# Tiny softmax instructions moved to ScalarE, and the first pairs' sums made by TensorE products

## The chip, the cores and the metric

The kernel runs on one core of a Trainium2 chip. The metric is the device time of one execution in microseconds; before the change the median of three runs is 959.35 us (959.06 to 961.71). Engines are named by their usual names: TensorE (PE in the profile; PEld is its weight load), VectorE (DVE), ScalarE (ACT), GpSimd (POOL) and the queue of SyncE (SP), which issues the DMAs.

## The reference

Three stages over 2304 tokens (4 batches of 576, 8 heads of 64 channels). The attention adds a coarse and a local part; then come two feed-forward layers.

```
q_d, k_d, v_d = means of q, k, v over groups of 4 tokens        # 144 of 576
out_d   = softmax(scale * q_d k_d^T) v_d ;  out_up = repeat(out_d, 4)
out_loc = softmax(scale * q k^T where |i - j| < 4, else -1e9) v
attn    = out_up + out_loc              # each softmax divides by (sum + 1e-9)
x = (h - tanh(h)) @ w_out,   h = attn @ w_in                      # 512 -> 2048 -> 512
y = (sigmoid(x @ w_gate) * (x @ w_val)) @ w_out2                  # 512 -> 1536 -> 512
```

All of it is fp32 in and out.

## The kernel before, in words

**Tiles and order.** Two heads make a pair (128 partitions); a pair is called (batch, number), and there are 16 of them. The tokens are also cut in six chunks of 384 for the first feed-forward layer, where for each chunk 16 blocks `f` of `h` (`do_h`, lines 650 to 658) and of `y` (`do_y`, 660 to 672) follow each other, `y` two blocks behind. Each block is 4 by 3 wide products (128x384), since weights and activations are split in a high and a low part (`mm3`, 283). The weights `w1` come in as 64-bit words, and ScalarE and VectorE make the two parts from them (`w_begin` 224, `w_bits` 236, `w_high` 244, `w_low` 254).

**Attention items.** The attention is a list of items (560 to 571): `("d", pair)` is the coarse part of a pair (`down`, 353), `("l", pairs, block)` the local part of six blocks of 64 tokens (`local`, 431). An item issues its first products at once and puts the rest on later steps: `down` the maximum 2 steps later (`top`), the exponentials 3 (`exps`), the division 5 (`normalise`, 340), the transposes 7 and 8 (`turn`), the products with v 10 (`values`).

**Steps.** `tick` (140) counts steps; `defer`, `chain` and `later` file work under a step. An h or y block is two steps. In the first chunk (`dense[0]`) `work` (763) starts item i when step `begin + 60 * (i - first) / (goal - first)` has come and the item before has had its 4 ("d") or 6 ("l") steps (`item`, 594). `fetch` (582) loads the next pair when the sums of the last have been taken up (`means`), and files their sums four steps later (`load_pair`, 318). Before the dense part of chunk 1 the loop at 938 steps on until all attention output of that chunk is stored.

**Sums of four tokens.** For a pair, `mean_qk` (324) makes the sums of q and k in one tile `m`: batch 0 by one VectorE reduction (328), the others by three GpSimd additions (330 to 332). `mean_v` (334) makes the sums of v with three GpSimd additions from the buffer `vr` (one for all pairs) into `vd`. `down` multiplies the summed q by the summed k (364) and the exponentials by the summed v (415). An fp32 product is two instructions in the profile.

**Tiny instructions.** In `down`, `top` ends with a VectorE product that scales the negated maxima, `nb` (383, 128x3). `normalise` begins with a VectorE instruction that adds 1e-9 to the sums and multiplies them (342, 128x3 or 128x6), then the reciprocal (346) and the product (348).

**The start.** Until the four x tiles of chunk 0 exist (742 to 757) each round issues unused products with the identity (`keep_warm`, 735; line 738): two at its head and, while fewer than eight items have been started, two more. The rest of each round is one item, some early h products and two steps. The place `spot` (697) holds q and k of pair (0,3) in its first 1152 of 4096 columns.

**Who keeps what order.** GpSimd keeps the program's order at the start (692), SP in chunk 0 (927), SP, ScalarE, VectorE and GpSimd in chunks 1 to 5 (929). TensorE is ordered by the compiler's scheduler up to the end of the first layer, ScalarE and VectorE up to the end of chunk 0. The kernel runs what is in each queue in its order.

Of the kernel before, what the change touches and what calls it, by code (L numbers as in the profile page):

```python
# [7 lines left out]
F32 = mybir.dt.float32  # L8
# [4 lines left out]
ACTF = mybir.ActivationFunctionType  # L13
ALU = mybir.AluOpType
AX = mybir.AxisListType
# [3 lines left out]
B, H, S, D = 4, 8, 576, 64  # L19
NP = H // 2  # L20
FAC = 4
SD = S // FAC
# [7 lines left out]
WIN = QB + 2 * (FAC - 1)  # L30
LB = 6
# [27 lines left out]
def tile_kernel(ctx: ExitStack, tc: tile.TileContext, qk, vp, v, w1, w2, mask, ident, out):  # L59
    nc = tc.nc  # L60
    scale = 1.0 / float(D) ** 0.5
# [11 lines left out]
    ap = pool("ap", 1, p1)  # L73
# [15 lines left out]
    startup, dense, spare = [True], [True], [0]  # L89
# [4 lines left out]
    def a_bank():  # L94

        spare[0] += 1
        if startup[0] and spare[0] % 5 == 2:
            return acc_bank(1)
        return ps.tile([128, 512], F32, tag="ab", bufs=4, name="ab")
# [6 lines left out]
    now = [0]  # L106
# [23 lines left out]
    def chain(n, fn, *args):  # L130

        chains.setdefault(now[0] + n, []).append(fn(*args))
# [156 lines left out]
    qks, means, vds, outd = {}, {}, {}, {}  # L289
# [20 lines left out]
        nc.sync.dma_start(out=qks[u], in_=qk[u[0], u[1]])  # L310

    def load_v(u):
        vds[u] = ap.tile([72, 2, 128], F32, tag="vd", bufs=2, name="vd")
        vr = ap.tile([72, 2, FAC, 128], F32, tag="vr", name="vr")
        nc.sync.dma_start(out=vr, in_=vp[u[0], u[1]])
        return vr

    def load_pair(u, d):
# [2 lines left out]
        defer(d, mean_qk, u)  # L321
        defer(d, mean_v, u, vr)

    def mean_qk(u):
        m = means[u] = ap.tile([128, 2, SD], F32, tag="m", bufs=1, name="m")
        t = qks[u].rearrange("p i (j r) -> p i j r", r=FAC)
        if u[0] == 0:
            nc.vector.tensor_reduce(out=m, in_=t, op=ALU.add, axis=AX.X)
        else:
            nc.gpsimd.tensor_tensor(out=m, in0=t[:, :, :, 0], in1=t[:, :, :, 1], op=ALU.add)  # L330
            nc.gpsimd.tensor_tensor(out=m, in0=m, in1=t[:, :, :, 2], op=ALU.add)
            nc.gpsimd.tensor_tensor(out=m, in0=m, in1=t[:, :, :, 3], op=ALU.add)

    def mean_v(u, vr):
        vd = vds[u]
        nc.gpsimd.tensor_tensor(out=vd, in0=vr[:, :, 0, :], in1=vr[:, :, 1, :], op=ALU.add)
        nc.gpsimd.tensor_tensor(out=vd, in0=vd, in1=vr[:, :, 2, :], op=ALU.add)
        nc.gpsimd.tensor_tensor(out=vd, in0=vd, in1=vr[:, :, 3, :], op=ALU.add)

    def normalise(pt, ssum, n, w, mul):  # L340
        r = ssum
        nc.vector.tensor_scalar(
            out=r, in0=ssum, scalar1=1e-9, scalar2=mul, op0=ALU.add, op1=ALU.mult
        )
        yield
        nc.vector.reciprocal(out=r, in_=r)
        yield
        nc.vector.tensor_tensor(
            out=pt, in0=pt, in1=r.unsqueeze(2).to_broadcast([128, n, w]), op=ALU.mult
        )  # L350


    def down(u):
        m = means.pop(u)
        qd, kd = m[:, 0, :], m[:, 1, :]
        four = not startup[0]
        sd = score_banks(3 * SD, 2 * SD, SD)
        place = [(j % 2, j // 2) if four else (0, j) for j in range(3)]
        for j in range(3):
            for h in range(2):  # L360
                r0 = 64 * h
                t, at = place[j]
                o0 = 64 - r0 if t else r0
                nc.tensor.matmul(  # L364
                    out=sd[t][o0:o0 + 64, at, :], lhsT=qd[r0:r0 + 64, 40 * j:40 * j + 64],
                    rhs=kd[r0:r0 + 64, :], start=True, stop=True,
                )
        sc = scale / (FAC * FAC)
        nb = ap.tile([128, 3], F32, tag="nb", bufs=2, name="nb")
        pd = ap.tile([128, 3, SD], F32, tag="pd", bufs=1, name="pd")  # L370
        ssum = ap.tile([128, 3], F32, tag="ss", bufs=2, name="ss")
        pdt = ap.tile([72, 2, 2, 3, 48], F32, tag="pdt", name="pdt")
        b, p = u
        if p % 2 == 0:
            outd[b, p // 2] = ap.tile([128, 2, SD], F32, tag="od", bufs=2, name="od")
        od = outd[b, p // 2]

        def top():
            for t in range(len(sd)):
                at = nb[:, t::2] if four else nb  # L380
                nc.vector.tensor_reduce(out=at, in_=sd[t], op=ALU.max, axis=AX.X, negate=True)
                yield
            nc.vector.tensor_scalar_mul(nb, nb, sc)

        def exps():
            for j in range(3):
                nc.scalar.activation(
                    out=pd[:, j, :], in_=sd[place[j][0]][:, place[j][1], :], func=ACTF.Exp, bias=nb[:, j:j + 1], scale=sc,
                    accum_out=ssum[:, j:j + 1],
                )  # L390

        def turn(f):
            if f == 0:
                defer(1, run_later, "d")
            tb = a_bank()[:72, :384]
            for j in range(3):
                nc.tensor.transpose(  # L397
                    out=tb[:, 128 * j:128 * j + 128], in_=pd[:, j, 72 * f:72 * f + 72], identity=id_sb
                )

            if not four:
                kept = bass.AP(tensor=tb.tensor, offset=tb.offset, ap=[list(tb.ap[0]), [64, 2], [136, 3], [1, 48]])
                defer(1, copy, pdt[:, f], kept)
                return
            outer = bass.AP(tensor=tb.tensor, offset=tb.offset, ap=[list(tb.ap[0]), [64, 2], [272, 2], [1, 48]])
            defer(1, copy, pdt[:, f, :, ::2, :], outer)
            for h in range(2):
                defer(1, copy, pdt[:, f, h, 1, :], tb[:, 200 - 64 * h:248 - 64 * h])

        def values():  # L410
            vd = vds.pop(u)
            ob = a_bank()[:, :SD]
            for h in range(2):
                for f in range(2):
                    nc.tensor.matmul(  # L415
                        out=ob[64 * h:64 * h + 64, :], lhsT=vd[:, f, 64 * h:64 * h + 64],
                        rhs=pdt[:, f, h].rearrange("p j k -> p (j k)"), start=(f == 0), stop=(f == 1),
                    )
            defer(1, copy, od[:, p % 2, :], ob)

        chain(2, top)
        defer(3, exps)
        chain(5, normalise, pd, ssum, 3, SD, float(FAC))
        wait = 0 if dense[0] else 2
        defer(7, turn, 0)
        defer(8, turn, 1)
        later("d", 10 + wait, values)

    def local(us, n):
        b, p = us[0]
# [5 lines left out]
        for x in (0, 3, 1, 4, 2, 5):  # L438
            i, j = blocks[x]
            t = qks[us[i]]  # L440
            w0 = win_start(j)
            for h in range(2):
                r0 = 64 * h
# [3 lines left out]
                    out=bank[o0:o0 + 64, at, :], lhsT=t[r0:r0 + 64, 0, QB * j:QB * j + QB],  # L447
                    rhs=t[r0:r0 + 64, 1, w0:w0 + WIN], start=True, stop=True,
# [6 lines left out]
        pl = ap.tile([128, LB, WIN], F32, tag="pl", bufs=2, name="pl")  # L455
        nb = ap.tile([128, LB], F32, tag="nl", bufs=2, name="nb")
        ssum = ap.tile([128, LB], F32, tag="sl", bufs=2, name="ss")
# [46 lines left out]
        def exps():  # L504
            for j in range(LB):
                nc.scalar.activation(  # L506
                    out=pl[:, j, :], in_=pl[:, j, :], func=ACTF.Exp, bias=nb[:, j:j + 1],
                    accum_out=ssum[:, j:j + 1],
                )

        def turn(f):
            if f == 0:
# [39 lines left out]
        defer(1, load_window)  # L552
        chain(2, top)
        defer(3, exps)
        chain(7, normalise, pl, ssum, LB, WIN, 1.0)
        defer(9, turn, 0)
        defer(10, turn, 1)
        later("l", 12, values)
# [35 lines left out]
    def item():  # L594

        fetch()
        x = items[started[0]]
        if x[0] == "d" and x[1] not in means:
            return 0
        started[0] += 1  # L600
        run_later()
        if x[0] == "d":
            down(x[1])
            return 4 if dense[0] else 7
        local(*x[1:])
        return 6 if dense[0] else 7
# [94 lines left out]
    vr = load_v((0, 0))  # L701
# [33 lines left out]
    def keep_warm(n):  # L735

        for _ in range(n):
            nc.tensor.matmul(out=idle[:, :128], lhsT=id_sb, rhs=id_sb, start=True, stop=True)  # L738
# [1 line left out]
    idle = acc_bank(0)  # L740
    free, rounds = [0], 0
    while any(((1, 0), k) not in xt for k in range(KD)):
        keep_warm(2)
        if started[0] < n_first:
            x = items[started[0]]
            item()
            if x[0] == "d":
                next_pair(x[1][1])
        early_h(2)
        tick()  # L750
        if started[0] < n_first:
            keep_warm(2)
        w_load(min(loaded[0] + 1, 3))
        rounds += 1
        if rounds % 3 == 0:
            w_begin(U1)
        tick()
# [388 lines left out]
```

## Time and profile before

| | us |
|---|---|
| median of three runs | 959.35 (959.06 to 961.71) |
| the profiled execution | 960.45 |
| its span, first to last instruction | 958.6 |
| TensorE busy | 934.3 (97%) |
| VectorE busy | 548.4 (57%) |
| ScalarE busy | 433.2 (45%) |
| GpSimd busy | 104.1 (11%) |

The profile is of one execution. A row of the time-line gives the start in us, the length in us, the engine, the line and the operation, the tile written and the tiles read, and in brackets the time that the engine had stood idle and what ended it. TensorE's instructions overlap: each lasts longer than the distance to the next one's start. The granted clock of TensorE is given as a share of 2.4 GHz, 0.5 being the lower of its two levels.

### The profile page before, as it was taken

The numbers are of one execution on the slowest core, as the hardware profiler recorded it, in microseconds if no ns is written. First come the engines' busy times: TensorE is split into PE (matmuls) and PEld (weight loads), VectorE is DVE, ScalarE is ACT, GpSimd is POOL, SyncE is SP. The second block draws the span as 40 slices with busy tenths as digits, with TensorE's granted clock in tenths as the row PEclk, the third lists the DMA queues.
The fourth block names the chain that finished last, engine by engine and source line by source line (L and its number), as shares of the span: only waits on it lengthen the run. The fifth ranks groups of instructions, "written<-read, shape, count | busy, mean of one in ns | idle before, by whom it ended". The sixth has DMA issues, their size and how long they took to land.

```text
span 958.6 us, 16060 instructions
## 1 busy us (share of the span) xinstructions
PE 934.3 (97%) x6260; PEld 867.8 (91%) x6260; DVE 548.4 (57%) x992; ACT 433.2 (45%) x1104; POOL 104.1 (11%) x113
## 2 busy tenths in 40 slices
PE   7888999999999999999999999999999998999998
PEld 6677989999999989999999999999999997888886
DVE  6897966344443534474346578585777676532231
ACT  4875755444543444452344545344443544422131
POOL 2243130302212020000033210000000000000000
PEclk9898999999999999999999999999999999999999
DMA  8475643212323120430121223142231445444341
GB/s 281 143 243 174 238 118 114 71 33 73 89 64 88 54 76 12 147 122 25 48 68 59 67 99 136 52 154 88 100 118 73 150 179 188 122 139 125 115 132 66
DMA packets 49963, 106.53 MB, mean 111 GB/s; under 512 B 5136, under 2 KB 35552, under 8 KB 45536
## 3 DMA queue, kind: packets, MB, share of 16 engines
q1 hardware_dynamic: 49888, 105.51, 33.3%
q8 instruction: 49, 0.80, 0.4%
q14 instruction: 26, 0.21, 0.1%
HBM read 77.97 MB, written 27.53 MB: 110 GB/s over the span
## 4 chain that ended last, share of the span: by engine, by line
PE 88%; DVE 3%; ACT 3%; DMA 2%; POOL 2%; issue 1%; SPq 0%; ACTq 0%; POOLq 0%; DVEq 0%
PE ab L284 14%; PE ab L286 14%; PE ab L285 14%; PE acc L284 13%; PE acc L285 12%; PE acc L286 12%; PE ab L525 2%; PE ab L446 1%; PE ab L516 1%; PE ab L397 1%; PE acc L738 1%; DMA qk<-in_qk 1%; PE ab L415 1%; PE ab L364 1%; ACT pl L506 1%
## 5 line engine op out<-in xcount | busy, mean ns | idle before, releaser
L297 DVE TENSOR_TENSOR t<-ab,t 128x384 f32<-128x384 f32 x94 | 52.2, 556 | 150.6 <-ACT t L640 150.4
L284 PE MATMUL acc<-g,w 128*128 128x384 f32 x384 | 133.2, 348 | 0.0
L284 PE MATMUL ab<-x,w 128*128 128x384 f32 x376 | 131.5, 350 | 1.2 <-DVE t L297 0.7
L285 PE MATMUL acc<-g,w 128*128 128x384 f32 x384 | 129.6, 337 | 0.0
L286 PE MATMUL acc<-g,w 128*128 128x384 f32 x384 | 129.5, 337 | 0.0
L285 PE MATMUL ab<-x,w 128*128 128x384 f32 x376 | 127.2, 338 | 0.0
L286 PE MATMUL ab<-x,w 128*128 128x384 f32 x376 | 127.2, 338 | 0.0
L640 ACT ACTIVATE t<-ab 128x384 f32<-128x384 f32 x94 | 45.8, 487 | 156.4 <-PE ab L286 155.3
L284 PE MATMUL acc<-x,f 128*128 128x384 f32 x252 | 84.8, 336 | 0.0
L286 PE MATMUL acc<-x,f 128*128 128x384 f32 x252 | 84.6, 336 | 0.0
L286 PE MATMUL ab<-x,f 128*128 128x384 f32 x252 | 84.6, 336 | 0.0
L285 PE MATMUL acc<-x,f 128*128 128x384 f32 x252 | 84.6, 336 | 0.0
L284 PE MATMUL ab<-x,f 128*128 128x384 f32 x252 | 84.6, 336 | 0.0
L285 PE MATMUL ab<-x,f 128*128 128x384 f32 x252 | 84.6, 336 | 0.0
L297 DVE TENSOR_TENSOR g<-t,g 128x384 fp32r<-128x384 f32 x96 | 59.8, 624 | 42.4 <-ACT g L294 40.1
L279 DVE TENSOR_TENSOR g<-u,g 128x384 fp32r<-128x384 f32 x72 | 38.6, 556 | 66.0 <-ACT g L294 65.9
L284 PEld LDWEIGHTS ab<-x,w 128*128 128x128 f32 x376 | 71.2, 189 | 4.5 <-issue 1.6
L284 PEld LDWEIGHTS acc<-g,w 128*128 128x128 f32 x384 | 72.2, 188 | 2.7 <-issue 1.8
L285 PEld LDWEIGHTS acc<-g,w 128*128 128x128 f32 x384 | 72.5, 189 | 0.3 <-issue 0.2
L286 PEld LDWEIGHTS acc<-g,w 128*128 128x128 f32 x384 | 72.3, 188 | 0.3 <-issue 0.2
L285 PEld LDWEIGHTS ab<-x,w 128*128 128x128 f32 x376 | 71.4, 190 | 0.0
L286 PEld LDWEIGHTS ab<-x,w 128*128 128x128 f32 x376 | 71.3, 189 | 0.1
(137 smaller groups left out, 1878.7 us busy)
## 6 DMA issues: line engine op xcount, KB each, us to landing
raw<-in_w SPq DMA_DIRECT2D x34, 1024.0 KB
u<-c SPq DMA_DIRECT2D x36, 384.0 KB
u<-u SPq DMA_DIRECT2D x72, 192.0 KB
qk<-in_qk SPq DMA_DIRECT2D x16, 576.0 KB
vr<-in_vp SPq DMA_DIRECT2D x16, 288.0 KB
y<-y SPq DMA_DIRECT2D x24, 192.0 KB
xs<-y SPq DMA_DIRECT2D x24, 192.0 KB
out<-o SPq DMA_DIRECT2D x17, 256.0 KB
```

The source lines that it names most:

```text
L279: nc.vector.tensor_tensor(out=dst[:, 1, :], in0=src, in1=dst[:, 0, :].bitcast(F32), op=ALU.subtract)
L284: nc.tensor.matmul(out=o, lhsT=wh, rhs=xh, start=first, stop=False, **kw)
L285: nc.tensor.matmul(out=o, lhsT=wh, rhs=xl, start=False, stop=False, **kw)
L286: nc.tensor.matmul(out=o, lhsT=wl, rhs=xh, start=False, stop=last, **kw)
L297: nc.vector.tensor_tensor(out=dst, in0=a, in1=b, op=ALU.subtract)
L364: nc.tensor.matmul(out=sd[t][o0:o0 + 64, at, :], lhsT=qd[r0:r0 + 64, 40 * j:40 * j + 64], rhs=kd[r0:r0 + 64, :], start=True, stop=True,)
L397: nc.tensor.transpose(out=tb[:, 128 * j:128 * j + 128], in_=pd[:, j, 72 * f:72 * f + 72], identity=id_sb)
L415: nc.tensor.matmul(out=ob[64 * h:64 * h + 64, :], lhsT=vd[:, f, 64 * h:64 * h + 64], rhs=pdt[:, f, h].rearrange("p j k -> p (j k)"), start ...
L446: nc.tensor.matmul(out=bank[o0:o0 + 64, at, :], lhsT=t[r0:r0 + 64, 0, QB * j:QB * j + QB], rhs=t[r0:r0 + 64, 1, w0:w0 + WIN], start=True, ...
L506: nc.scalar.activation(out=pl[:, j, :], in_=pl[:, j, :], func=ACTF.Exp, bias=nb[:, j:j + 1], accum_out=ssum[:, j:j + 1],)
L525: nc.tensor.matmul(out=ob[r0:r0 + 64, QB * x:QB * x + QB], lhsT=vw[0][:, j - n, i, r0:r0 + 64], rhs=pt[:, x, o0:o0 + 64], start=True, stop ...
L640: nc.scalar.activation(out=t, in_=hb[:, :N], func=ACTF.Tanh)
```

## The change

- The scale of `nb` and the guard of the sums become ScalarE activations (`Copy` with a scale and a bias), issued with the exponentials.
- For batch 0 `mean_v` does nothing, and `values` multiplies by the four unsummed v of each group and accumulates: 8 products per head where there were 2. The v of pairs (0,1) and (0,2) get a place of their own in `spot`.
- For pairs (0,1) to (0,3) `mean_qk` sums k only, and `down` multiplies the four unsummed q of each group by the summed k and accumulates: 24 products where there were 6.
- In the first chunk a "d" item is not started until five steps after its sums were issued.
- `keep_warm` issues two products at a round's head until three items have been started and one from then on, and two more in a round only until then.

```diff
     def load_v(u):
-        vds[u] = ap.tile([72, 2, 128], F32, tag="vd", bufs=2, name="vd")
-        vr = ap.tile([72, 2, FAC, 128], F32, tag="vr", name="vr")
+        if u[0] == 0 and u[1] in (1, 2):
+            vr = vds[u] = spot[:72, 2 * S + 1024 * (u[1] - 1):2 * S + 1024 * u[1]].rearrange(
+                "k (f r c) -> k f r c", f=2, r=FAC
+            )
+        else:
+            vr = ap.tile([72, 2, FAC, 128], F32, tag="vr", name="vr")
+            vds[u] = vr if u[0] == 0 else ap.tile([72, 2, 128], F32, tag="vd", bufs=2, name="vd")
...
     def mean_qk(u):
+        summed[u] = now[0]
...
         if u[0] == 0:
-            nc.vector.tensor_reduce(out=m, in_=t, op=ALU.add, axis=AX.X)
+            first = 1 if u[1] else 0
+            nc.vector.tensor_reduce(out=m[:, first:], in_=t[:, first:], op=ALU.add, axis=AX.X)
...
     def mean_v(u, vr):
+        if u[0] == 0:
+            return
...
-    def normalise(pt, ssum, n, w, mul):
+    def guard(ssum, mul):
+        nc.scalar.activation(out=ssum, in_=ssum, func=ACTF.Copy, scale=mul, bias=1e-9 * mul)
+
+    def normalise(pt, ssum, n, w):
         r = ssum
-        nc.vector.tensor_scalar(
-            out=r, in0=ssum, scalar1=1e-9, scalar2=mul, op0=ALU.add, op1=ALU.mult
-        )
-        yield
...
-        for j in range(3):
+        whole = qks[u][:, 0, :].rearrange("p (j r) -> p r j", r=FAC)
+        spread = u[0] == 0 and u[1] > 0
+        for j in range(3) if spread else ():
+            for r in range(FAC):
+                for h in range(2):
+                    r0 = 64 * h
+                    nc.tensor.matmul(
+                        out=sd[0][r0:r0 + 64, j, :], lhsT=whole[r0:r0 + 64, r, 40 * j:40 * j + 64],
+                        rhs=kd[r0:r0 + 64, :], start=(r == 0), stop=(r == FAC - 1),
+                    )
+        for j in range(3) if not spread else ():
...
-            nc.vector.tensor_scalar_mul(nb, nb, sc)
 
         def exps():
+            nc.scalar.activation(out=nb, in_=nb, func=ACTF.Copy, scale=sc)
             for j in range(3):
...
+            guard(ssum, float(FAC))
...
+            parts = [(f, r) for f in range(2) for r in range(FAC)] if u[0] == 0 else [(0, None), (1, None)]
             for h in range(2):
-                for f in range(2):
+                for x, (f, r) in enumerate(parts):
+                    vt = vd[:, f, :] if r is None else vd[:, f, r, :]
                     nc.tensor.matmul(
-                        out=ob[64 * h:64 * h + 64, :], lhsT=vd[:, f, 64 * h:64 * h + 64],
-                        rhs=pdt[:, f, h].rearrange("p j k -> p (j k)"), start=(f == 0), stop=(f == 1),
+                        out=ob[64 * h:64 * h + 64, :], lhsT=vt[:, 64 * h:64 * h + 64],
+                        rhs=pdt[:, f, h].rearrange("p j k -> p (j k)"), start=(x == 0), stop=(x == len(parts) - 1),
                     )
...
-        if x[0] == "d" and x[1] not in means:
+        if x[0] == "d" and (x[1] not in means or now[0] < summed[x[1]] + (5 if dense[0] and not startup[0] else 0)):
             return 0
...
-        keep_warm(2)
+        keep_warm(2 if started[0] < 3 else 1)
...
         if started[0] < n_first:
-            keep_warm(2)
+            keep_warm(2 if started[0] < 3 else 0)
```

In `local`, `exps` likewise ends with `guard(ssum, 1.0)`.

## Rows read from the trace of the kernel before

**Rows 1.** The page, part 1: busy time, share of the span, instructions.

```profile
PE 934.3 (97%) x6260; PEld 867.8 (91%) x6260; DVE 548.4 (57%) x992; ACT 433.2 (45%) x1104; POOL 104.1 (11%) x113
```

**Rows 2.** Busy by stretch: from:to, length, PE, PEld, DVE, ACT, POOL, granted clock, DMA.

```profile
50.00:126.00 76.00, 67.55 (x599) 59.48 (x599) 68.57 (x110) 52.06 (x147) 27.50 (x24) 0.96 0.59 199
22.00:29.30 7.30, 7.30 (x104) 5.58 (x104) 7.12 (x14) 5.53 (x18) 3.35 (x3) 1.00 0.55 168
29.30:37.00 7.70, 4.73 (x61) 3.54 (x61) 6.35 (x15) 7.70 (x36) 3.06 (x3) 0.86 0.70 235
37.00:50.00 13.00, 13.00 (x121) 10.00 (x121) 10.15 (x15) 10.77 (x18) 0.00 (x0) 0.82 0.38 123
...
70.40:82.60 12.20, 7.97 (x56) 7.12 (x56) 7.81 (x13) 4.51 (x11) 4.15 (x4) 0.72 0.50 172
82.60:126.00 43.40, 41.85 (x380) 36.94 (x380) 41.30 (x66) 33.51 (x96) 13.43 (x12) 1.00 0.56 190
...
146.50:700.00 553.50, 552.53 (x3849) 535.13 (x3848) 305.12 (x590) 244.49 (x652) 60.46 (x66) 1.00 0.24 79
```

**Rows 3.** Waits of TensorE: who waited for whom, us in total, times, longest.

```profile
PE ab L364 <- POOL m L332: 4.2, 1, 4.2
PE ab L525 <- ACT pt L294: 3.0, 2, 2.6
PE ab L516 <- DVE pl L348: 1.9, 1, 1.9
```

**Rows 4.** Time-line of TensorE and GpSimd, 69 to 75.8 us.

```profile
69.97 0.49 PE L516 MATMUL ab<-id_sb,pl 128*70 128x128 f32 x3
74.69 0.71 PE L364 MATMUL ab<-m 64*64 64x144 f32 x12 [4.23 <-POOL m L332]
...
73.69 0.94 POOL L332 TENSOR_TENSOR m<-m,qk 128x288 f32<-128x288 f32 x1
```

**Rows 5.** Time-line of TensorE: two wide products that follow each other.

```profile
144.47 0.34 PE L284 MATMUL ab<-x,w 128*128 128x384 f32 x1
144.65 0.34 PE L285 MATMUL ab<-x,w 128*128 128x384 f32 x1
```

**Rows 6.** Lines 342, 383: ns min/median/max; busy 50:126 (342, then 383); neighbours.

```profile
L342 DVE TENSOR_SCALAR ss<-ss x40: 155/164/1584, 10.4 to 389.8; 128x6 f32<-128x6 f32 x24, 128x3 f32<-128x3 f32 x16
...
L383 DVE TENSOR_SCALAR nb<-nb x16: 158/273/735, 8.7 to 356.8; 128x3 f32<-128x3 f32 x16
...
50.00:126.00 76.00, 4.34 (x8) 0.96 0.59 199
...
50.00:126.00 76.00, 1.55 (x3) 0.96 0.59 199
...
58.11 0.93 DVE L342 TENSOR_SCALAR ss<-ss 128x6 f32<-128x6 f32 x1
...
L695 ACT ACTIVATE z<-z 128x1 f32<-128x1 f32 x1 | 0.2, 203 | 0.0
```

**Rows 7.** The start: VectorE's sums by line, then time-line and chain.

```profile
L328 DVE TENSOR_REDUCE m<-qk 128x288 f32<-128x1152 f32 x4 | 5.4, 1349 | 6.6 <-DMA qk<-in_qk 4.9 <-PE acc L364 1.5
...
18.12 0.95 PE L364 MATMUL acc<-m 64*64 64x144 f32 x12
...
22.43 0.74 PE L415 MATMUL ab<-pdt,vd 72*64 72x144 f32 x8
...
29.29 0.41 ACT L294 ACTIVATE pdt<-ab 72x288 f32<-72x288 f32 x1 [1.40 <-PE ab L397]
...
39.02 0.99 PE L284 MATMUL acc<-x,w 128*128 128x384 f32 x2
...
19.07 3.10 PE acc L738 x26
```

**Rows 8.** Weight loads by line and shape: busy us, mean ns; 64 and 128 columns.

```profile
L364 PEld LDWEIGHTS acc<-m 64*64 64x64 f32 x24 | 1.4, 132 | 0.3 <-ACT pd L387 0.3
...
L285 PEld LDWEIGHTS acc<-g,w 128*128 128x128 f32 x384 | 72.5, 189 | 0.3 <-issue 0.2
```

More of the change, by code (lines that the diff above doesn't have):

```diff
@@ L322, in load_pair @@
         defer(d, mean_v, u, vr)
+    summed = {}
     def mean_qk(u):
+        summed[u] = now[0]
         m = means[u] = ap.tile([128, 2, SD], F32, tag="m", bufs=1, name="m")
@@ L422, in down @@
         defer(3, exps)
-        chain(5, normalise, pd, ssum, 3, SD, float(FAC))
+        chain(5, normalise, pd, ssum, 3, SD)
         wait = 0 if dense[0] else 2
@@ L509, in exps @@
                 )
+            guard(ssum, 1.0)
         def turn(f):
@@ L554, in local @@
         defer(3, exps)
-        chain(7, normalise, pl, ssum, LB, WIN, 1.0)
+        chain(7, normalise, pl, ssum, LB, WIN)
         defer(9, turn, 0)
```

## The prediction

> **What bounds the kernel now.** I read the page's head first, then busy time by stretch, then TensorE's list of waits, then the time-line around the longest of them. The head: TensorE is busy 934.3 of 958.6 us [rows 1], so almost every microsecond is TensorE work, and a change can win only where TensorE idles, runs at the lower clock, or multiplies something nobody uses. The stretches show where that is. From 146.5 to 700 us TensorE is busy 552.53 of 553.50 us at full clock [rows 2]: nothing that only touches VectorE or ScalarE there can move the end. All the room lies in the first 126 us. Two stretches there have a granted clock below 1, and since the clock has two levels (1.2 and 2.4 GHz) the time at the lower one can be worked out: (1 - 0.72) x 12.20 / 0.5 = 6.8 us in 70.4 to 82.6, and (1 - 0.86) x 7.70 / 0.5 + (1 - 0.82) x 13.00 / 0.5 = 6.8 us between 29.3 and 50.
>
> Three waits stand out [rows 3]: 4.2 us for GpSimd's `m` (the summed q and k of a pair), 2.6 us for a ScalarE copy, 1.9 us for a VectorE normalisation. The first two precede the two falls of the clock. The time-line of the first shows the mechanism [rows 4]: TensorE has issued its last transposes at 69.97, next in its queue are the products of pair (1,1), and they wait until GpSimd's last addition (73.69, 0.94 long) ends. TensorE takes its queue in order, so the wide products behind stood still too. In 82.6 to 126 VectorE is busy 41.30 of 43.40 us beside TensorE's 41.85 [rows 2]: that stretch has two bounds close together, and what TensorE wins earlier can be taken back there.
>
> **Part 1: five steps from sums to products.** Counting steps through the planner's code: in the first chunk ten items are spread over 60 steps, six apart. Pair (1,0) has its sum in step 53 and its products in 60: untouched. Pair (1,1) has both in step 65; now its products wait for step 70. The items behind it move by three (74, 80, 86; (1,2) in 92, already 15 steps behind its sum, now 17). (1,3) is summed in 97 and multiplied in 102 (before: 94 and 95), and the last item of the chunk moves from 101 to 106, the loads of chunk 1 from step 116 to 121. A step is half an h or y block, six wide products; they start 0.18 apart [rows 5], so 1.1 us. Five steps put 5.4 us of products into a hole of 4.2 us: the wait goes (-4.2), and with it the fall of the clock, 6.8 us in which TensorE did half of what it could (-3.4). The steps added at the end of the chunk hold no dense work of their own; blocks 14 and 15 and the last y blocks can be drawn ahead, since TensorE is not kept to program order here. SP is kept to it: the load of chunk 1 stays behind the last item's store and the weight loads stay behind that load, so if the cover is too thin the start of chunk 1 is late. I take 0 and keep +3 for the range.
>
> **Part 2: tiny instructions to ScalarE.** L342 (40 of them) and L383 (16) leave VectorE. Their median is 164 and 273 ns, but the longest took 1584 and 735 [rows 6]: in 50 to 126 eight and three of them took 4.34 + 1.55 = 5.9 us, 0.54 each. On ScalarE the nearest row is the 128x1 activation, 0.20 us; with both the guard and the scale waiting for the value just before them I take 0.2 to 0.4 each. After 126 us this is all hidden by TensorE. In 50 to 126 VectorE loses 5.9 us and ScalarE gains 11 x 0.2 to 0.4 = 2 to 4 us, and ScalarE has the room (33.51 of 43.40 us busy [rows 2]). The wait of 1.9 us for the normalisation [rows 3] had an L342 of 0.93 us (58.11) queued ahead on VectorE [rows 6]: -0.9. Another -0.5 for the smaller waits of that kind. What is queued behind the new instructions: the exponentials of the same item behind the scale, the next copy on ScalarE behind the guard, the reciprocal on VectorE behind both.
>
> Here a rule speaks against the change. The Trainium skill (ScalarE: Activation LUTs, section "Rules for kernel authors") says that additions and multiplications belong on VectorE and not on ScalarE. At the medians the rows agree with it (0.16 against 0.20); at the mean of the stretch that counts, 0.54, they do not. By the rule the part would be worth nothing, 0 in place of -1.4, and the sum below 1.4 higher.
>
> **Part 3: first pairs' sums by products.** Removed: 12 GpSimd additions at the start, on no TensorE wait; half of three VectorE reductions of 1349 ns [rows 7], -2.0 us of VectorE; with the twelve tiny ones of the first 50 us VectorE is relieved of some 4.5 us there. The loads of v no longer wait for GpSimd; for (0,1) and (0,2) they have a place of their own, for (0,3) the load waits for the value products of (0,0), about when it waited for GpSimd before. The loads keep their number on SP. Added on TensorE: each product is two instructions, so q of three pairs goes from 12 to 48 (+108), values of four pairs from 8 to 32 (+96). Twelve of the first took 0.95 us and eight of the second 0.74 [rows 7], that is 0.08 and 0.09 each with the tail of the last one counted in, about 0.05 without (a wide product lasts 0.34 though the next starts 0.18 later [rows 5]). At 0.06: 204 x 0.06 = 12.2 us. Counting the rounds, the unused products fall from 42 to 20, 44 instructions less; 26 took 3.10 us [rows 7], so 44 x 0.12 = -5.3 us. Net +6.9 us of TensorE.
>
> How much shows? The chain runs on TensorE up to the pdt copy at 29.29, for which ScalarE had idled 1.40 [rows 7]. Up to 22 the extra q products of (0,2) (36 x 0.06 = 2.2) stand where unused ones stood (3.10): nothing. From there to 29.3 come q of (0,3) and the values of (0,0) and (0,1): 84 x 0.06 = 5.0 us, less gaps that I can't see exactly. VectorE, 7.12 of 7.30 us busy there [rows 2], gives back part: what TensorE's transposes wait for comes earlier. Bounds: -2 (all hidden, VectorE's relief shows) to +7 (all of the net shows). I take **+2.5**, nearer the middle because the copy at 29.29 is reached through both engines. The fall of the clock after the wait of 2.6 us I leave as it is: the wait may move, but I see no reason why it must vanish.
>
> The strided weights have no row. Below: nothing, as a load of 64 columns (132 ns) hides behind the products. Above: as if each cost what 128 columns cost, 189 ns [rows 8]: 144 loads x 0.057 / 2 (two halves of the array side by side) = +4. I take 0, since the loads overlap the products, and keep +4 for the range.
>
> **The sum**, for the profiled execution (960.45 us, of which 958.6 are span): -4.2 - 3.4 - 1.4 + 2.5, and +1.5 given back where VectorE is the second bound (68.6 of 76 us busy before [rows 2]; 62.7 of some 67 then) = **-5.0**. That execution lies 1.1 above the median of the runs; against the median, 959.35 - 5.0 = **954.3**. A measurement of this kernel can tell about 0.3% from no change, 2.9 us: 956.5 to 962.2 counts as the same.
>
> **The rivals.**
>
> *A, slower: the start becomes TensorE's.* All 6.9 us of part 3 show and the strided loads add 4: +10.9, against -7.5 from the rest, gives 962.8. For it: TensorE shows no idle time from 22 to 29.3 [rows 2]. Against: much of that is unused products, and the chain after 29.3 is ScalarE's. It decides if the first x products, now at 39.02 [rows 7], begin more than 10 us later. A rule points the same way: the Trainium skill (SBUF — State Buffer, section "Door 1: The DMA port swizzle") says that accesses that go to a new 16-byte line each time pay a penalty, which is how q would be read; it gives no figure for it, and no run here shows it. Chance 0.13.
>
> *B, the same: the gain is swapped for another wait.* Either the five steps are too few (GpSimd finishes over 1 us later than before and TensorE waits again), or the stretch from 82.6 becomes VectorE's: half of the 7.6 comes back. -3.8 - 0.9 + 2.5 = -2.2, 957.2. For it: VectorE's 95% in that stretch. Against: it is relieved of 5.9 us. Part of this is that the rule does little: it moves two of four pairs, and only one of them had a wait. Chance 0.21.
>
> *C, faster than forecast.* The products of part 3 fill the hole of 2.6 us, so that the first fall of the clock goes too (-2.6 - 3.4), nothing is given back, and the start's cost stays at +2.5 to +4: -4.2 - 3.4 - 1.4 - 6.0 + 4.0 = -11.0, 948.3. For it: the holes and the new work are neighbours. Against: the copy waited for is ScalarE's, and ScalarE gets more work there. Chance 0.20.
>
> **How the numbers follow.** The forecast proper (951 to 956.5) has the remaining 0.46. Faster by over 0.3%: forecast and C, 0.66; within: B, 0.21; slower: A, 0.13. The range leaves out most of A and the far half of C: 948 to 962.
>
> **What would show it.** Right: no wait of L364 for `m` over 1 us, no clock below 1 between 60 and 126, L342 and L383 gone from VectorE with 0.2 to 0.4 each on ScalarE, GpSimd's first addition after 50 us, the first x products at 39 to 44. Wrong: the first x products after 46, a new wait on L364 or at chunk 1's first products, a second fall of the clock left in place.

## The result and the profile after

| | before | after |
|---|---|---|
| median of four runs each, us | 960.53 (959.06 to 962.08) | 972.16 (971.24 to 973.6) |
| ratio, 95% interval | | 1.0117 [1.0094, 1.014] |
| the profiled execution, us | 960.45 | 973.6 |
| its span, us | 958.6 | 971.8 |

The change made the kernel 1.2% slower, 11.6 us, where 5 us less were forecast. The page's head after, to be read against [rows 1]:

```profile
PE 951.3 (98%) x6422; PEld 885.5 (91%) x6422; DVE 532.3 (55%) x936; ACT 444.0 (46%) x1160; POOL 92.6 (10%) x101
```

VectorE and GpSimd are relieved as intended (16.1 and 11.5 us less), and TensorE is busy 17 us longer. Busy time by stretch, columns as in [rows 2]: from:to, length, PE, PEld, DVE, ACT, POOL, granted clock, DMA share, GB/s:

```profile
29.30:37.00 7.70, 7.70 (x109) 7.01 (x106) 5.11 (x7) 5.06 (x8) 0.00 (x0) 1.00 0.73 261
37.00:50.00 13.00, 11.00 (x91) 8.93 (x90) 10.00 (x19) 9.12 (x41) 0.00 (x0) 0.64 0.38 116
50.00:70.40 20.40, 20.40 (x152) 17.61 (x150) 6.86 (x9) 8.79 (x16) 0.00 (x0) 0.65 0.04 11
82.60:126.00 43.40, 40.78 (x344) 37.22 (x343) 39.53 (x58) 32.93 (x91) 14.02 (x12) 0.96 0.73 244
146.50:700.00 553.50, 550.46 (x3854) 531.29 (x3853) 297.96 (x557) 254.38 (x700) 62.60 (x69) 1.00 0.24 80
...
40.50:64.40 23.90, 23.73 (x126) 20.11 (x128) 10.00 (x17) 12.54 (x37) 0.00 (x0) 0.50 0.15 50
```

The row to read first is the last: from 40.5 to 64.4 us the granted clock is at its lower level (1.2 GHz) without a break, and TensorE is busy 23.73 of these 23.90 us. Before, the clock was low for 6.8 us in that part of the span. Half of 23.9 us, 12 us of full-speed work, is lost there. The other thing to see is the fourth column: in 50 to 70.4 VectorE works 6.86 us of 20.40 (19.46 of 20.40 before), and its longest wait there, 8.1 us, is for TensorE (line 549). The start has become TensorE's.

TensorE's time-line of the start says with what, and ahead of what the clock fell (times are start and length; in brackets the idle time before and what ended it):

```profile
19.46 3.22 PE L375 MATMUL acc<-m,qk 64*64 64x144 f32 x48
23.06 3.70 PE L438 MATMUL ab<-pdt,vr 72*64 72x144 f32 x32
...
37.23 0.92 PE L549 MATMUL ab<-pt,vw 70*64 70x64 f32 x24
39.03 0.52 PE L540 MATMUL ab<-id_sb,pl 128*70 128x128 f32 x3 [0.88 <-DVE xs L564]
40.67 0.85 PE L418 MATMUL ab<-id_sb,pd 128*72 128x128 f32 x3 [1.12 <-DVE pl L521]
...
46.28 5.12 PE L438 MATMUL ab<-pdt,qk 72*64 72x144 f32 x24
51.33 1.01 PE L284 MATMUL acc<-x,w 128*128 128x384 f32 x2
...
53.55 7.04 PE L438 MATMUL ab<-pdt,vr 72*64 72x144 f32 x32
```

Line 438 holds the value products (415 before). A pair's 32 (instructions, two to a product) take 3.70 us at full clock, 0.116 each, where the eight of before took 0.74 in all [rows 7]; at the lower clock they take 7.04. The q products (375) take 3.22 for 48, 0.067 each. Between 38 and 41 us two waits of 0.88 and 1.12 us leave TensorE mostly idle, and the clock falls behind them. The first x products begin at 51.33 instead of 39.02 [rows 7].

TensorE's waits, to be read against [rows 3]:

```profile
PE ab L469 <- ACT pd L407: 2.4, 1, 2.4
PE ab L418 <- DVE pd L358: 1.8, 1, 1.8
PE ab L418 <- DVE pl L521: 1.1, 1, 1.1
PE ab L540 <- DVE xs L564: 0.9, 1, 0.9
```

The wait of 4.2 us for GpSimd's `m` is gone, as forecast. In its place, at 101.3, is one of 2.4 us for an exponential, with a second fall of the clock (3.4 us) behind it.

Comparing start times of the same product in both time-lines: the first x product is 12.3 us late, block 13 of chunk 0 9.2 (137.6 against 128.4), the second block of chunk 1 14.3 (165.7 against 151.4), the span's end 13.2. So something is won back between 51 and 138 us, and some 5 us are lost where chunk 1 starts, with a wait of 1.8 us for VectorE (the second row above, at 148.6) among them.

### The profile page after: what moved, and what is told of

It is laid out like the page before. It is cut to its first block, busy times and chain, and to the rows that moved or that the text cites. A ratio compares the mean times of both kernels' runs of the same rounds, so it can differ in the third digit from the quotient of the medians.

```text
span 971.8 us, 16345 instructions
## 1 busy us (share of the span) xinstructions
PE 951.3 (98%) x6422; PEld 885.5 (91%) x6422; DVE 532.3 (55%) x936; ACT 444.0 (46%) x1160; POOL 92.6 (10%) x101
## 4 chain that ended last, share of the span: by engine, by line
PE 89%; DMA 4%; DVE 3%; ACT 3%; issue 1%; SPq 0%; ACTq 0%; DVEq 0%
PE ab L284 14%; PE ab L286 14%; PE ab L285 14%; PE acc L284 13%; PE acc L285 13%; PE acc L286 12%; PE ab L438 2%; DMA raw<-in_w 2%; PE ab L549 2%; PE ab L540 1%; PE ab L469 1%; PE ab L418 1%; PE ab L384 1%; PE acc L375 1%; DMA u<-u 1%
## 5 line engine op out<-in xcount | busy, mean ns | idle before, releaser
L297 DVE TENSOR_TENSOR g<-t,g 128x384 fp32r<-128x384 f32 x96 | 60.3, 629 | 45.3 <-ACT g L294 43.1
```

The source lines that it names most:

```text
L297: nc.vector.tensor_tensor(out=dst, in0=a, in1=b, op=ALU.subtract)
```

## The experiments

Twelve kernels, in three groups of four, each group on one chip beside the kernel before (medians there 959.28, 960.88 and 961.44 us). Since the chips differ a little, kernels are compared by their ratio to before; 0.1% is 1 us. The last column takes the clock out: the median over the runs of time - (1 - mean granted clock) x span, that is, an estimate of the time if the stretches at 1.2 GHz had run at 2.4 and all their work were TensorE's. By it the kernel before is at 952.4, 952.3 and 952.9 in the three groups: its clock costs it 7 to 8.5 us.

| kernel | median us | ratio [95%] | at full clock, us |
|---|---|---|---|
| after | 972.16 | 1.0117 [1.0094, 1.014] | 960.7 |
| v sums undone | 953.01 | 0.9938 [0.9916, 0.9961] | 950.2 |
| values in alternation | 958.48 | 0.9995 [0.9966, 1.0023] | 954.2 |
| unused products undone | 959.20 | 1.0000 [0.9983, 1.0016] | 958.5 |
| five steps undone | 969.48 | 1.0104 [1.0083, 1.0125] | 958.7 |
| v sums and unused products undone | 949.90 | 0.9900 [0.9864, 0.9936] | 949.8 |
| alternation, unused products undone | 955.05 | 0.9943 [0.9921, 0.9964] | 955.0 |
| v sums and five steps undone | 956.31 | 0.9965 [0.9938, 0.9993] | 951.2 |
| before + five steps | 955.04 | 0.9961 [0.9939, 0.9984] | 950.3 |
| unused products late | 958.81 | 0.9979 [0.9958, 0.9999] | 958.3 |
| unused products in the middle | 966.18 | 1.0065 [1.0036, 1.0093] | 957.5 |
| before + tiny + five steps | 955.49 | 0.9936 [0.9914, 0.9958] | 948.5 |
| v sums, unused products, five steps undone | 955.09 | 0.9942 [0.9915, 0.997] | 953.0 |

### v sums undone

```diff
-        if u[0] == 0 and u[1] in (1, 2):
...
+        vds[u] = ap.tile([72, 2, 128], F32, tag="vd", bufs=2, name="vd")
+        vr = ap.tile([72, 2, FAC, 128], F32, tag="vr", name="vr")
...
-        if u[0] == 0:
-            return
...
-            parts = [(f, r) for f in range(2) for r in range(FAC)] if u[0] == 0 else [(0, None), (1, None)]
+            parts = [(0, None), (1, None)]
```

> The changed kernel with one part undone: v of the first four pairs is summed by GpSimd again and values has 8 instructions per pair. Theory 1 (the value products run one after the other, 32 of them in 3.70 us at full clock and 7.0 at the lower one, and push the start by 12 to 19 us): the first x products come before 42 us, the lower clock after 40 us lasts 7 us or less, time 956 to 961. Theory 2 (fewer unused products let the clock fall for 24 us): the long fall stays, time 966 to 970. Theory 3 (the loss is the five steps' at the start of chunk 1): the loss of 3 to 4 us between the last y blocks of chunk 0 and the first h block of chunk 1 stays; theory 1 and 3 can both hold.

It measured 0.9938: 1.8% or 17 us faster than the changed kernel, 0.6% faster than before, and 3 us below theory 1's figures. Its first x products begin at 36.77, and the clock is low for 3.4 us (37.0 to 40.5) and not again before the last 2 us of the span. The stretch that was at 0.64 with 0.65 behind it:

```profile
37.00:50.00 13.00, 12.90 (x126) 9.94 (x129) 9.28 (x16) 11.82 (x32) 0.00 (x0) 0.87 0.45 159
50.00:70.40 20.40, 18.00 (x184) 16.04 (x177) 19.69 (x28) 15.52 (x52) 12.30 (x11) 1.00 0.75 256
```

With the whole v part undone (the products, GpSimd's additions and the places of v together) the loss is gone; everything else in the change together beats the kernel before.

### Values in alternation

The 32 products stay, but the two heads' products follow each other in turn instead of 16 of one head and then 16 of the other.

```diff
-            for h in range(2):
-                for x, (f, r) in enumerate(parts):
-                    vt = vd[:, f, :] if r is None else vd[:, f, r, :]
+            for x, (f, r) in enumerate(parts):
+                vt = vd[:, f, :] if r is None else vd[:, f, r, :]
+                for h in range(2):
```

> The changed kernel with the two loops of values swapped (the eight parts outside, the two heads inside), the same 32 instructions per pair. Theory 1 in its sharper form (instructions of one head share the same 64 columns of the array and can't run side by side; those of the two heads can): 32 take about 2.0 us and not 3.70, the start comes 5 to 12 us earlier, time 961 to 967. If the scheduler or the engine had nothing to gain from the order: 3.70 us as before and 972.

The time-line has a pair's 32 in 2.18 us instead of 3.70:

```profile
22.63 2.18 PE L438 MATMUL ab<-pdt,vr 72*64 72x144 f32 x32
```

0.068 each, as the q products, which were emitted in turn from the start. So 0.116 is the price of an instruction in a row of 16 and 16, of which each 16 write the same 64 output partitions (one half of the array's columns), and 0.068 its price where the halves alternate. The Trainium skill (TensorEngine Tiling (Array Packing), section "Key Properties") says that tiles operate independently, so that different ones can load weights and multiply in parallel. The runs agree, at 0.068 against 0.116, but 16 of one half in a row do not reach the other half's. Four in a row do: a later pair's eight, emitted as four and four, take as long as eight that alternate (the first line is of the kernel with the unused products alone undone, the second of the one with alternation and these undone):

```profile
84.93 0.72 PE L438 MATMUL ab<-pdt,vd 72*64 72x144 f32 x8
```

```profile
78.47 0.71 PE L438 MATMUL ab<-pdt,vd 72*64 72x144 f32 x8
```

The time is that of the kernel before, 0.9995, under the 961 to 967 that was expected, with the widest spread of all (954.66 to 967.85 over ten runs). The spread is the clock's: at a mean granted clock of 1.0 the runs take about 955, at 0.994 959, and the profiled one, at 0.986, 967.85, with the clock low from 39.1 to 62.9 us. Clock taken out, all lie within 953 to 956.

### Unused products undone

```diff
-        keep_warm(2 if started[0] < 3 else 1)
+        keep_warm(2)
...
-            keep_warm(2 if started[0] < 3 else 0)
+            keep_warm(2)
```

> The changed kernel with the unused products of the kernel before (42 in place of 20). Theory 2: the clock stays up or falls for 7 us, 8 to 9 us come back, 963 to 965. Theory 1: the 44 instructions cost their own time (0.12 each, 5.3 us at most) or fit in holes; the long fall stays, 971 to 977.

```profile
37.00:50.00 13.00, 13.00 (x162) 11.95 (x160) 11.45 (x20) 10.87 (x43) 0.00 (x0) 1.00 0.36 117
50.00:70.40 20.40, 19.88 (x210) 17.62 (x208) 13.32 (x23) 15.33 (x46) 2.86 (x4) 1.00 0.34 99
```

Ratio 1.0000, 11 us faster than the changed kernel and below what either theory gave, though TensorE does 21 products more that nobody uses (84 instructions of that line and not 42): the clock stays at 1.00, and the value products still take 3.70 us for a pair. Clock taken out, 958.5 against 960.7: the saved products saved nothing even then. Two causes thus hold at once, and the next run asks whether they are one.

### v sums and unused products undone

Both edits together.

> The changed kernel with both suspects undone at once: the first pairs' v sums back on GpSimd (8 value products for a pair) and the unused products back to 42. With the three kernels already timed (both new 972.2, v sums undone 953.0, unused products undone 959.2) it is the fourth corner of a square. Theory 1 (the two losses are one: the unused products matter only because the long rows of value products leave TensorE's clock in reach of a fall, so with 8 value products the unused ones are worth no more than their own time): 953 to 957, slower than with v sums undone alone by 0 to 4 us, and no stretch at the low clock. Theory 2 (the unused products are worth 13 us whatever stands beside them): about 940 to 942. Theory 3 (each is only a price of its own, the value products 19 us): no different from 953 by more than 1 us, with the 3.4 us at the low clock still there.

949.90, ratio 0.9900 [0.9864, 0.9936], four runs within 1.3 us, clock 0.999 to 1.0: faster than both kernels, and the best of the study. It lies 3 us below theory 1's figures and 8 above theory 2's; theory 1 had it slower than with the v sums alone undone, and it isn't. There is no low stretch, which goes against theory 3. Against before the four corners are

| | 42 unused products | 21 unused products |
|---|---|---|
| 8 value products a pair | -9.6 us | -6.0 us |
| 32 value products a pair | 0.0 us | +11.2 us |

(ratio less 1, times 960). The value products cost 9.6 us where the clock holds and 17.2 where it doesn't; leaving out unused products costs 3.6 us beside short rows of value products (the two intervals overlap) and 11.2 beside long ones. So there are two prices, and each makes the other larger. What they add to each other is for the most part the clock: with it taken out the corners are at 949.8 and 950.2 (8 value products), 958.5 and 960.7 (32), so that the value products cost 8.7 or 10.5 and the missing unused products 0.4 or 2.2.

### Alternation, unused products undone

> The changed kernel with 32 value products for a pair, but in an order in which the two heads' products stand beside each other (0.067 us each instead of 0.115), and with the 42 unused products back. Theory 1 (two separate prices, 0.115 us for each value product in a row and the clock's fall when TensorE is left short of work at the start): against the kernel with the unused products alone undone (959.2) it saves 3 pairs x 32 x 0.048 = 4.6 us: 954 to 956, clock full throughout, one tight group of times. Theory 2 (the spread of the kernel with the order alone changed, 954.7 to 967.9, is something other than the clock): the spread stays, over 5 us.

0.9943, within 953.5 to 956.5, clock full. The spread is gone with the unused products back, so it was the clock. Against the corner at 1.0000 alternation saves 5.5 us; the expectation's 4.6 counted three pairs, and by all four it is 4 x (3.70 - 2.18) = 6.1. The rest of the way to the corner at 0.9900 is 4.1 to 5.2 us (by ratio, by the last column), against 4 x (2.18 - 0.74) = 5.8 that the rows give. The value products' own price is thus read from rows to within some 2 us.

### Unused products late, and in the middle

Of the 21 missing unused products ten come back in the last rounds, or nine in the rounds of items four to six. (The traces have 62 and 60 instructions of that line, two to a product, and 42 in the changed kernel; the second expectation counts eleven.)

```diff
-        keep_warm(2 if started[0] < 3 else 1)
+        keep_warm(2 if started[0] < 3 or started[0] >= n_first else 1)
...
-            keep_warm(2 if started[0] < 3 else 0)
+            keep_warm(2 if started[0] < 3 or started[0] >= 6 else 0)
```

(late; in the middle both conditions are `started[0] < 6`, with 1 and 0 as before.)

> The changed kernel with 31 unused products instead of 21 (before: 42): ten come back in the last rounds, after the sixth item has been started, none in between. If what matters is that the holes around 38 to 43 us, just ahead of the long rows of value products, are filled (theory 1), these ten do nearly all of what the 21 did: 958 to 962, clock full or low for under 7 us. If what matters is the total or the middle of the start (theory 2): 966 to 972, with a stretch of over 15 us at the low clock.

> The changed kernel with 32 unused products: eleven come back in the rounds of the fourth to sixth item, and none more in the last rounds. The counterpart of the run before. By theory 1 (the holes at 38 to 43 us are what lets the clock fall) it stays at 966 to 973 with over 15 us at the low clock; by theory 2 (the number, or the middle) 958 to 964.

Late: 0.9979, clock 0.999 to 1.0 in all ten runs. In the middle: 1.0065; in nine of its ten runs the mean clock is 0.986 to 0.991, and the profiled one has it low from 45.3 to 62.4; the tenth keeps it at 1.0 and takes 959.77. So the place decides most of it: ten late are worth 13 us against the changed kernel's 1.0117, nine in the middle some 5. The time-line of the first, over the microseconds in which the changed kernel had its two waits:

```profile
38.04 0.92 PE L549 MATMUL ab<-pt,vw 70*64 70x64 f32 x24
38.89 2.05 PE L762 MATMUL acc<-id_sb 128*128 128x128 f32 x16
40.77 0.49 PE L540 MATMUL ab<-id_sb,pl 128*70 128x128 f32 x3
41.25 0.52 PE L418 MATMUL ab<-id_sb,pd 128*72 128x128 f32 x3
41.84 0.92 PE L549 MATMUL ab<-pt,vw 70*64 70x64 f32 x24
42.59 1.15 PE L438 MATMUL ab<-pdt,qk 72*64 72x144 f32 x8
43.66 0.45 PE L284 MATMUL acc<-x,w 128*128 128x384 f32 x1
```

The products of lines 549, 540 and 418 are those of the changed kernel, in its order. Eight unused products (16 instructions, 2.05 us) fill the hole, and no low stretch follows. The scheduler also draws x products ahead to 43.66, but that is later than 40.5, where the changed kernel's clock fell, so it is not what keeps the clock. It may be part of what keeps it afterwards; that was not told apart.

### The five steps

Undone in the changed kernel, undone beside the v sums, undone beside v sums and unused products, and alone in the kernel before (there the line goes in, the other way round):

```diff
-        if x[0] == "d" and (x[1] not in means or now[0] < summed[x[1]] + (5 if dense[0] and not startup[0] else 0)):
+        if x[0] == "d" and x[1] not in means:
```

> The changed kernel without the five steps. Theory 3 (the rule loses 4 to 5 us at the start of chunk 1 and wins 7.6 at pair (1,1)): TensorE waits for m again by 3 to 5 us with a fall of the clock after it, the loss at chunk 1 goes, time 973 to 977. If the rule wins nothing because the start now differs: 966 to 970.

> The changed kernel with the v sums back on GpSimd and without the five steps between sums and products. What is left against before: tiny instructions on ScalarE, q's first pairs by products, fewer unused products. Theory 1 (the wait of the first chunk-1 pair's products for GpSimd's sums comes back when GpSimd does v sums again, as in the kernel before, and the five steps are what removes it): 956 to 961, 3 to 8 us slower than with the v sums alone undone (953.0), with a wait of 2 to 4 us of TensorE on GpSimd near 70 us. Theory 2 (the wait went because the sums now start sooner, and the five steps only delay): 949 to 952, no such wait.

> The changed kernel with v sums on GpSimd, 42 unused products and without the five steps: what is left is tiny instructions and q by products. Against the same kernel with the five steps (949.9, no wait for GpSimd's sums, clock full) it shows what the five steps are worth once the start keeps its clock. Theory 1 (they take away the wait of 3 to 4 us for GpSimd's sums near 70 us and the low clock behind it, 3.4 us long): 954 to 957, with that wait and that stretch there. Theory 2 (their gain is eaten by lateness at the start of chunk 1, as the 2.7 us of the run without them suggested): 948 to 951.

> The kernel before with the five steps between sums and products, nothing else. Theory 1 (the rule takes away the 4.2 us wait for GpSimd's sums and the second fall of the clock after it, as the prediction had it): 7.6 us less than before, less what lateness costs: 951 to 954. Theory 2 (the rule's lateness at the start of chunk 1, 2.7 us in the changed kernel, eats what the wait gave, and the clock's second fall has another cause): 957 to 961. In both the first fall at 35 to 42 us stays.

- In the changed kernel: 1.0104 against 1.0117, not told apart from no difference. Without the rule TensorE doesn't wait for `m` at all there.
- Beside the v sums: 0.9965 against 0.9938, 2.6 us worse, with overlapping intervals. The wait is back, at 3.1 us where [rows 3] had 4.2, and so is a low stretch of 3.4 us behind it (71.6 to 75). The wait, and the stretch around it:

```profile
PE ab L377 <- POOL m L336: 3.1, 1, 3.1
```

```profile
70.40:82.60 12.20, 11.06 (x83) 9.15 (x84) 10.23 (x17) 6.84 (x21) 1.08 (x2) 0.86 0.44 153
```

- Beside v sums and unused products: 0.9942 against 0.9900, 4.0 us worse (the intervals overlap a little), the time of theory 1 without its mechanism: the wait for `m` is only 0.5 us, two others of 2.0 us for VectorE end at 42.5 and 125.7, the clock is low from 42.8 to 53.0, and the mean clock of its ten runs goes from 1.0 down to 0.989. The profiled run is the second longest of the ten; clock taken out, some 3 of the 4.0 us stay, and where they come from was not found.
- Alone in the kernel before: 0.9961, 3.7 us better, between the two theories. The wait for `m` is gone, but a shorter one for VectorE has come in its place, much as rival B had it, and a low stretch at 74.1 stays behind that, of 3.4 us where before had 6.8:

```profile
73.86 0.58 PE L411 MATMUL ab<-id_sb,pd 128*72 128x128 f32 x3 [1.77 <-DVE pd L352]
```

What the trace shows of why the changed kernel doesn't need the rule: GpSimd makes the three additions of (1,1) in a row and ahead of that pair's v sums, 2.95 us from first to last. Before, v additions came first and one stood between them, and the three took from 69.84 to 74.63 (the last of them in [rows 4]). Which part of the change gave GpSimd this order was not tested alone. GpSimd in the kernel with the five steps undone:

```profile
80.74 0.70 POOL L339 TENSOR_TENSOR m<-qk 128x288 f32<-128x288 f32 x1 [2.43 <-PE ab L384]
81.52 0.94 POOL L340 TENSOR_TENSOR m<-m,qk 128x288 f32<-128x288 f32 x1
82.54 1.15 POOL L341 TENSOR_TENSOR m<-m,qk 128x288 f32<-128x288 f32 x1
83.65 1.73 POOL L347 TENSOR_TENSOR vd<-vr 72x256 f32<-72x256 f32 x1
```

The rule's own price is at the start of chunk 1. From block 13 of chunk 0 to the second block of chunk 1, the ten kernels with the rule lose 1.9 to 6.5 us on the kernel before (5.1 the changed one, 3.2 the rule alone, 2.1 the best), the three without it 0.5 to 0.8.

### Before + tiny + five steps

The changed kernel with q, v and unused products all as before.

> The kernel before with the tiny instructions on ScalarE and the five steps between sums and products, nothing of the change at the first pairs: q and v summed by VectorE and GpSimd, 42 unused products. Against the kernel that also has q by products (949.9) it gives the price or gain of q by products, against the five steps alone (955.0) the gain of the tiny instructions. By the prediction's terms (tiny instructions 1.4 us, q's products 6.5 us of TensorE less what VectorE's relief gives) 951 to 955, and q by products is worth -1 to -4. By the rival that q's products cost what they add: 945 to 948. By the rival that the tiny instructions alone make the whole gain over the five steps: 949 to 951.

0.9936, 2.4 us better than the five steps alone, with overlapping intervals, about what the prediction's terms gave. Clock taken out it has the shortest time of the study, 948.5, but its clock is low in three stretches of the profiled run (6.8, 3.4 and 3.4 us). With q by products on top (the best kernel, 0.9900) TensorE has more to do, 949.8 clock taken out, and the clock no longer falls: by the ratios q by products is worth 3.5 us, though it adds work; the intervals overlap, so that this gain is not told apart from nothing.

## Why the prediction was wrong

**The step that failed first is the price of a value product.** Part 3 took 0.06 us for each of the 204 added instructions, from rows of twelve and eight instructions in which the halves of the array run side by side. For the q products it held: 0.067. The value products are emitted 16 for one head and then 16 for the other, and took 0.116. For four pairs that is 4 x (3.70 - 0.74) = 11.8 us where the sum had 96 x 0.06 = 5.8. The eight value products that it read, 0.74 in rows 7, have the head outside too, but four of a head in a row, and such a row is as short as one in alternation (0.72 and 0.71). So the row could not show the price; the step that failed was to carry a price from rows of four and four to rows of 16 and 16. The start's cost, taken as +2.5 with +7 as its upper bound, is 9.6 us for the v part where the clock holds.

**The second is the unused products.** The sum took their time off, 44 x 0.12 = -5.3 (42 went and not 44), and left "the fall of the clock" as it was, with no reason seen "why it must vanish". Nothing was asked about the other direction, that it could grow. It grew from 6.8 to 23.9 us, half of which is lost. Their real worth is measured with ten of them back in the right place: -13 us against the changed kernel (0.9979 against 1.0117), more than twice the 5.3 us at which the sum priced all of them. In the text they are called unused; by these runs they hold the clock while the attention items wait for each other.

**The forecast of the sum.** Clock taken out, the changed kernel takes 960.7 and before 952.4: 8.3 us more work and waits. The clock adds the remaining 3.4 (11.5 lost after, 8.1 of 960.53 before). The prediction had -5.0 for both together, and in it -3.4 for the clock. Put in one after the other, by ratio, the five steps give -3.7, the tiny instructions -2.4, q by products -3.5, fewer unused products +3.6 and v by products +17.2, together the +11.2 measured; only the first and the last of these are clear of the noise by themselves.

**The five steps.** -4.2 for the wait and -3.4 for the clock were right in mechanism where GpSimd's work is as before: the rule alone takes away the wait, and half of the low stretch behind it; a wait of 1.77 us for VectorE takes its place. Its lateness at chunk 1, taken as 0 with 3 as a bound, is 3.2 us there and 5.1 in the changed kernel; alone it is worth 3.7 and not 7.6. In the changed kernel it is worth nothing that can be measured, since the wait is gone without it; the prediction added the parts as if each met the kernel before.

**The tiny instructions.** On ScalarE they take 0.2 us each with hardly any spread, the lower end of the 0.2 to 0.4 taken:

```profile
L352 ACT ACTIVATE ss<-ss x40: 192/206/214, 10.8 to 399.5; 128x6 f32<-128x6 f32 x24, 128x3 f32<-128x3 f32 x16
...
L405 ACT ACTIVATE nb<-nb x16: 187/205/254, 9.3 to 370.0; 128x3 f32<-128x3 f32 x16
```

On VectorE they took up to 1584 and 735 ns [rows 6]. The forecast gain, 1.4, stands beside a measured 2.4 on top of the five steps, within what these runs can tell. The Trainium skill's rule against additions and products on ScalarE (ScalarE: Activation LUTs, section "Rules for kernel authors") would have made it 0; the runs lean to the other side but don't exclude it.

**The strided weights**, taken at 0 with +4 as a bound, cost nothing in time that shows: 0.067 us for a product with strided weights (q) against 0.068 for one with contiguous weights (v in alternation). The loads themselves did become as long as the upper bound had them, 190 ns and not 132 [rows 8]:

```profile
L375 PEld LDWEIGHTS acc<-m,qk 64*64 64x64 f32 x96 | 6.1, 190 | 0.2 <-ACT pd L407 0.2
```

The Trainium skill (SBUF — State Buffer, section "Door 1: The DMA port swizzle") gives a penalty for accesses to new 16-byte lines, a reason for rival A. The length of these loads agrees with it, at 190 against 132 ns; the products, no further apart for it, hide the loads, as the prediction had taken it.

**The rivals.** Rival A, the start becomes TensorE's, is what happened, at a chance of 0.13. Its point of decision, first x products over 10 us late, was met: 12.3. Its price of 962.8 was too low by 9 us: it had 5.8 us for value products that took 11.8, 4 for strided loads that cost nothing, and nothing for the clock. The list of what would prove the forecast wrong held: x products after 46 us, new waits around the start of chunk 1, a second fall of the clock (at 102). Three signs of being right came true as well and saved nothing: no wait for `m`, 0.2 us for each tiny instruction, GpSimd's first addition after 50 us (at 75.3).

## What to carry to other kernels

Price a row of small products by the order in which it is emitted and by how many of one half stand in a row: here two half-array streams shared the time when they alternated or came by fours, and not by sixteens. A price read from short rows holds for short rows. Before removing work that nobody uses, look at which holes it fills and what the granted clock does there, and count a stretch at the lower clock as half its length; here ten unused products at the end of the start were worth 13 us and nine in its middle 5. And parts of a change that attack the same wait are not to be added: price each against the kernel with the others in it, best as a square of four runs.

## What was unexpected of the hardware

- The clock fell with no TensorE wait longer than 1.12 us near it, while before it stayed full behind a wait of 1.9 us [rows 3] (at 62.3). So the length of one wait did not decide. It then stayed low for 23.9 us in which TensorE was busy 23.73; small transposes, value products of 72x64 and some ten wide products filled them. What ended that stretch was not tested.
- One source gives very different spreads by its clock alone: ten runs within 3 us with the holes filled (values in alternation, unused products back), over 13 us without (954.66 to 967.85).
- The same 32 value products take 3.70 us or 2.18 us by the order of two loops, with the same operands; for eight the order makes no difference (0.72 and 0.71).
- A weight load of 64 columns whose elements lie 16 bytes apart took 190 ns where a contiguous one took 132, and the products, 0.067 us apart, showed nothing of it.
